# Attention with head pairs as units, and its first outputs moved inside SBUF into the next layer's input

## The chip, the cores and the metric

The kernel runs on one core of one Trainium2 chip. What counts is the device time of one execution in microseconds (us); a "run" is the median of its executions. The core has five engines that work beside each other, each through its own list of instructions: PE (TensorE: matmuls and transposes; PEld is its loading of weights), DVE (VectorE), ACT (ScalarE), POOL (GpSimd) and SP (SyncE), which in this kernel issues every DMA. Sixteen DMA engines carry the transfers between DRAM and SBUF, the on-chip memory of 128 partitions.

## What is computed

Three stages follow each other: a gated linear attention over 4 batches, 8 heads, 768 time steps and head dimension 48; a layer with a rational function; a layer with a cosine.

```python
for t in range(S):                       # attention, per batch and head
    state = alpha[:, :, t, :, None] * state + einsum('bhd,bhe->bhde', k[:, :, t], v[:, :, t])
    y[:, :, t] = einsum('bhd,bhde->bhe', q[:, :, t], state)
x = y.transpose(0, 2, 1, 3).reshape(B * S, H * D)          # 3072 tokens x 384
h = x @ w_in                                               # layer 1, 384 x 2048
P = a0 + a1*h + a2*h**2 + a3*h**3;  Q = 1 + |b0|*|h| + |b1|*h**2
x = (P / (Q + 1e-6)) @ w_out
h = x @ w_in2                                              # layer 2
return (h * cos(h)) @ w_out2
```

## The kernel before

Time is cut into NC = 6 chunks of C = 128 steps. A unit is one chunk of one batch: u = 4c + b, NU = 24 units in all. A tile of a unit has 128 partitions, two heads of a pair in rows 0 to 47 and 64 to 111 (the other rows are padding), and along the free axis four head pairs (HP = 4) of 128 steps. One slot of the attention loop (n from -3 to 24) carries several units, each in another stage: DVE makes the running product of alpha (`decay`) and its inverse, POOL scales q (L303, `scale_q`) and k (L298, `scale_k`) and masks the two score tiles (L323, `mask1`), PE computes scores, state and output, ACT copies out of PSUM. Each slot also splits one weight tile of the layers into a high and a low part (ACT L70, L71 and L195, DVE L75 and L76, POOL L205), since every float32 product of a layer is made of three products of such parts.

The output of a unit is copied out of PSUM by ACT (L400, `y_out`). For the first four units (chunk 0), the high part is rounded in that copy and DVE subtracts it from the PSUM value for the low part (L406, `y_lo`). `y_store` (L416) writes both to a DRAM buffer `x0d` (name in the trace `x`), 256 KB each; for units 4 and up the whole value goes to DRAM as `x0d` (name in the trace). High and low parts rest until then in tiles `kept` (`g`) and in rows of layer 1's input tile `y_rest` (`x`).

Layer 1's input of a block (one chunk of all four batches: 512 tokens) is three tiles of 128 of the 384 columns (kk), high and low. For block 0 both parts are read back from DRAM by `x_pieces`: `x_load(0, 0, kk)` makes a list of eight DMAs, which the attention loop issues one per slot from n = 8 (L1307): four over 128 partitions (256 KB) and four over 64 (128 KB). Rows in SBUF are 512 B at a time, since batches lie apart in DRAM. For blocks 1 to 5, `x_load` (L675) issues four DMAs at once; then ACT (L680) and DVE (L684) split the tile. The columns of layer 1 stand in an order in which heads of one parity follow each other, and the host orders the rows of w_in the same way (`by_pairs`).

All DMAs stand in one queue of SP, in the order of the code: in a slot the stores (L416), then loads of `a` (alpha, 258 KB), `kq` (k and q, 512 KB), one raw weight (L156, 384 KB; `raw` or `spare`), `v` (192 KB), then the x piece. A DMA also waits for the one that was issued eight before it. Layer 1 starts while the last units of attention are still worked on (slots LEAD = 20 and up): PE's products b<-x,w (L537), then the rational function on ACT, DVE and POOL (L603 to L624), then the second product (L553).

The loop of slots, as far as it bears on DMAs, follows with the functions.

Of the kernel before, what the change touches and what calls it, by code (L numbers as in the profile page):

```python
# [2 lines left out]

# [1 line left out]

# [5 lines left out]
F32 = mybir.dt.float32  # L11
F32R = mybir.dt.float32r
# [5 lines left out]
B, H, S, D = 4, 8, 768, 48  # L18
DM, DFF = 384, 2048
NC, C = 6, 128  # L20
HP = 4
NF = DFF // 128
NK = DM // 128
TB = B * C
# [16 lines left out]
def attn_then_two_moe(ctx, tc, kqT, aT, vP, w1i, w1o, ma, mb, w2i, w2o, out):  # L41
    nc = tc.nc
# [2 lines left out]
    dram = ctx.enter_context(tc.tile_pool(name="dram", bufs=1, space=bass.MemoryType.DRAM))  # L45

    xd = [dram.tile([NC, B, 128 * HP, C], F32, name="x0d"), dram.tile([NC, DM, TB], F32, name="x1d")]
    x0d = dram.tile([2, B, 128 * HP, C], F32, name="x0")
    wd = dram.tile([2 * NF, 128, 2, DM], F32, name="wd")
    wf = dram.tile([NF, 128, DM], F32, name="wf")  # L50

# [34 lines left out]
    wp = main.enter_context(tc.tile_pool(name="w", bufs=1))  # L86
# [26 lines left out]
    v_t = [const.tile([128, H * D + 64 - D], F32, tag=f"v{i}", name=f"v{i}") for i in range(4)]  # L113
    st_all = const.tile([128, 4, DM], F32, tag="st", name="st")

    ws = [[wp.tile([128, 2, DM], F32R, tag=f"w{s}_{i}", name=f"w{s}_{i}") for i in range(NF)] for s in range(2)]
    s_all = [const.tile([128, HP * D + 64 - D], F32, tag=f"s{b}", name=f"s{b}") for b in range(B)]
    s_c = [s[:, :HP * D].rearrange("p (a b) -> p a b", a=HP) for s in s_all]

# [6 lines left out]
    ready = set()  # L126
    spare = x_p.tile([128, 2, NK, TB], F32R, tag="x", name="spare").rearrange("p a b c -> p (a b c)").bitcast(I32)
    xt = {(0, 0): x_p.tile([128, 2, NK, TB], F32R, tag="x", name="x")}
    y_rest = xt[0, 0].rearrange("p a b c -> p (a b c)")
    raw64 = {}  # L130
    stage = {}
    LEAD = NU - 4
# [258 lines left out]
    def y_out(u):  # L391
        d = U[u]
        if u < NU - B:
            d["yo"] = kept[2 + u % 2]
            if 2 <= u < B:
                d["yo"] = y_rest[:, (2 + u) * TB:(3 + u) * TB].bitcast(F32).rearrange("p (a t) -> p a t", a=HP)
        else:
            d["yo"] = in_p.tile([128, HP, C], F32, tag="p", name="yo")
        out = d["yo"].bitcast(F32R) if u < B else d["yo"]
        nc.scalar.activation(out=out, in_=d["y"], func=AF.Copy)  # L400

    def y_lo(u):
        d = U[u]
        d["lo"] = y_rest[:, u * TB:(u + 1) * TB]
        yo = d["yo"].rearrange("p a t -> p (a t)")
        nc.vector.tensor_tensor(  # L406
            out=d["lo"], in0=d["y"].rearrange("p a t -> p (a t)"), in1=yo, op=ALU.subtract
        )

    def y_store(u, rest=False):  # L410
        c, b = divmod(u, B)
        if rest:
            to, t = x0d[1, b], U[u]["lo"].bitcast(F32)
        else:
            to, t = xd[0][c, b] if c else x0d[0, b], U[u]["yo"].rearrange("p a t -> p (a t)")
        nc.sync.dma_start(out=to.rearrange("(p a) t -> p (a t)", a=HP), in_=t)  # L416

    def convert(n, place):

# [232 lines left out]
    def x_load(m, blk, kk):  # L652
        if kk == 0 and (m, blk) not in xt:
            xt[m, blk] = x_p.tile([128, 2, NK, TB], F32R, tag="x", name="x")
        x = xt[m, blk][:, 1, kk, :].bitcast(F32)
        ks = slice(kk * 128, (kk + 1) * 128)
        pieces = []
        if m:
            nc.sync.dma_start(out=x, in_=xd[1][blk, ks, :])
        else:  # L660
            gap = (64 - D) * HP
            for p, row in {0: [(slice(0, 128), 0)], 1: [(slice(0, 64), 128), (slice(64, 128), 192 + gap)],
                           2: [(slice(0, 128), 256 + gap)]}[kk]:
                to_from = [(x, xd[0][blk])] if blk else [
                    (xt[0, 0][:, i, kk, :].bitcast(F32), x0d[i]) for i in range(2)
                ]
                for to, of in to_from:
                    rows = of[:, row:row + p.stop - p.start, :]
                    pieces.append(partial(
                        nc.sync.dma_start,  # L670
                        out=to[p].rearrange("p (b t) -> p b t", b=B), in_=rows.rearrange("b p t -> p b t")
                    ))
        if blk or m:
            for piece in pieces:
                piece()  # L675
        return pieces

    def x_hi(m, blk, kk):
        x = xt[m, blk]
# [586 lines left out]
    with tc.manual_schedule():  # L1266
        nc.scalar.preload_act_table_set("natural_log_exp_and_others")
        for name, u in (("a", 0), ("kq", 0), ("a", 1), ("a", 2), ("kq", 1)):
            load(u, name)
        nc.vector.memset(fresh, P_MIN)  # L1270
        nc.gpsimd.memset(ones, 1.0)
        nc.gpsimd.memset(half_pi, HALF_PI)
        nc.gpsimd.memset(lnb, LN_S * ONE_EPS)
        for t in v_t:
            nc.gpsimd.memset(t[:, H * D:], 0.0)
        nc.gpsimd.memset(ident, 1.0)
        nc.gpsimd.affine_select(
            ident, ident, pattern=[[1, 128]], compare_op=ALU.is_equal, fill=0.0, base=0, channel_multiplier=-1
        )
        for s in s_all:  # L1280
            nc.gpsimd.memset(s[:, HP * D:], 0.0)
        warm_up(13)
        x_pieces = [p for kk in range(NK) for p in x_load(0, 0, kk)]
        for n in range(-3, NU + 1):
            slot[0] = n
            if n == -1:
                load(3, "a")
                load(1, "v")
            if n >= 2:
                y_store(n - 2)  # L1290
            if 0 <= n - 3 < B:
                y_store(n - 3, True)
            if n >= -1:
                load(n + 5, "a")
            if n >= 0:
                load(n + 3, "kq")
                for i in range((min(n, 1) if n not in (0, 20) else 2) if n <= LEAD else 0):
                    w_fetch(2 * NF)
                load(n + 2, "v")
            if n == 3:  # L1300
                nc.sync.dma_start(out=cab[:, 0:4], in_=ma.unsqueeze(0).to_broadcast([128, 4]))
                nc.sync.dma_start(out=cab[:, 4:6], in_=mb.unsqueeze(0).to_broadcast([128, 2]))
            if n == 6:
                nc.scalar.activation(out=cq[:, 0:2], in_=cab[:, 4:6], func=AF.Abs)
                nc.scalar.activation(out=cq[:, 2:6], in_=cab[:, 0:4], func=AF.Copy, scale=-LN_S * LN_S)
            if n >= 8 and x_pieces:
                x_pieces.pop(0)()  # L1307
            if n == 1:
                warm_up(8)
            attention(n)  # L1310
            if n == -3:
                for name, u in (("v", 0), ("kq", 2)):
                    load(u, name)
            w_lo([nc.gpsimd])
            if n >= LEAD:
                layers(n - LEAD)
                y_out(n - 1)
        y_store(NU - 1)
        for n in range(NU + 1 - LEAD, F0):
            layers(n)  # L1320
        for k in range(SLOTS):
            threes(k)
        acc_out()
# [3 lines left out]
    def general():  # L1327
# [12 lines left out]
        with tc.For_i(0, NC, 1) as c:  # L1340
# [14 lines left out]
            for t in range(C):  # L1355
                v = two.tile([128, B, HP, D], F32, name="v")
                for j in range(2):
                    for b in range(B):
                        row = vP[one, b, t].rearrange("o (a j e) -> o j a e", a=HP, j=2)[:, j]
                        nc.sync.dma_start(out=v[64 * j:64 * j + 64, b], in_=row.to_broadcast([64, HP, D]))  # L1360
                w = two.tile([128, B, HP, D], F32, name="w")
                at = a[:, :, :HP].unsqueeze(3) if t == 0 else a_rest[:, :, :, t:t + 1]
                nc.vector.tensor_tensor(out=state, in0=state, in1=at.to_broadcast([128, B, HP, D]), op=ALU.mult)
                nc.vector.tensor_tensor(out=v, in0=v, in1=over_e(k, t), op=ALU.mult)
                nc.vector.tensor_tensor(out=state, in0=state, in1=v, op=ALU.add)
                nc.vector.tensor_tensor(out=w, in0=state, in1=over_e(q, t), op=ALU.mult)
                y = two.tile([2, B, HP, D], F32, name="y")
                for i in range(2):
                    p = psf.tile([2, 2, HP, D], F32, name=f"yp{i}")
                    nc.tensor.matmul(p, half, w[:, 2 * i:2 * i + 2], start=True, stop=True)  # L1370
                    nc.vector.tensor_copy(y[:, 2 * i:2 * i + 2], p)
                rows = yd[t].rearrange("b (a j e) -> j b a e", a=HP, j=2)
                for b in range(B):
                    nc.sync.dma_start(out=rows[:, b], in_=y[:, b])
            for b in range(B):
                yh = two.tile([128, DM], F32, name="yh")
                nc.sync.dma_start(out=yh, in_=yd[:, b, :])
                y = two.tile([128, DM], F32, name="yt")
                nc.vector.tensor_copy(y.rearrange("p (e a) -> p e a", a=HP), yh.rearrange("p (a e) -> p e a", a=HP))
                for kk in range(NK):  # L1380
                    p = psf.tile([128, 128], F32, name="tp")
                    nc.tensor.transpose(p, y[:, kk * 128:(kk + 1) * 128], ident)
# [124 lines left out]
```

## Time and profile before

| | us |
|---|---|
| runs (three) | 916.93, 918.09, 919.14 |
| median | 918.09 |
| profiled execution | 916.58 |
| its span | 914.9 |
| PE busy | 893.7 (98% of the span) |
| POOL, DVE, ACT busy | 710.0, 703.8, 695.5 |
| attention, until PE works without a gap | about the first 130 |

The granted TensorE clock is full in the whole span. The gaps of PE lie in the attention part. The DMA engines are full for about the first 115 us and a third busy after that. To read the profile, take the attention part apart from the layers: the wait that ends last before PE's continuous work says what a change in the attention part can move.

### The profile page before, as it was taken

Reading aid. Unit: us, or ns where it says so; the run is one execution under the profiler, and the core shown is the slowest. Engines: PE = TensorE matmul, PEld = TensorE weight load, DVE = VectorE, ACT = ScalarE, POOL = GpSimd, SP = SyncE. Lnnn points to the kernel's source line nnn. Section 1 sums busy time; section 2 is a strip of 40 time slices with the busy share of each in tenths; the row PEclk is TensorE's granted clock in tenths of the full one; section 3 lists DMA queues with packets and bytes.
Section 4 is the critical chain, followed back from the end, with each engine's and each line's share of the span. In section 5 each row is a group of like instructions: output and inputs, shape, how many; then the busy total and the mean of one; then the engine's idle time right before and its main releaser. Section 6 shows DMA issues by size and latency. Waiting matters only on the chain.

```text
span 914.9 us, 15676 instructions
## 1 busy us (share of the span) xinstructions
PE 893.7 (98%) x5348; PEld 740.6 (81%) x5348; DVE 703.8 (77%) x1247; ACT 695.5 (76%) x1302; POOL 710.0 (78%) x699
## 2 busy tenths in 40 slices
PE   7899989999999999999999999999999999999997
PEld 6787767888888888888888888878888888888885
DVE  8998789999899989979979968666367554555552
ACT  6998888888879788878778878756577666666653
POOL 7999999989789979879879767758887475655332
PEclk9999999999999999999999999999999999999999
DMA  9999840100234132232165467530243432533432
GB/s 324 388 380 379 331 132 18 31 22 18 69 113 121 44 126 74 78 121 87 41 190 195 153 209 252 196 120 27 69 139 104 155 123 89 171 104 104 139 104 90
DMA packets 67305, 128.83 MB, mean 141 GB/s; under 512 B 6928, under 2 KB 30224, under 8 KB 67216
## 3 DMA queue, kind: packets, MB, share of 16 engines
q1 hardware_dynamic: 67216, 127.74, 41.4%
q8 instruction: 44, 0.72, 0.3%
q14 instruction: 45, 0.37, 0.1%
HBM read 95.21 MB, written 32.51 MB: 140 GB/s over the span
## 4 chain that ended last, share of the span: by engine, by line
PE 86%; ACT 6%; DMA 3%; DVE 3%; issue 2%; POOL 0%; SPq 0%; ACTq 0%; DVEq 0%
PE b L537 28%; PE acc L553 28%; PE acc L1032 15%; PE b L997 6%; PE r L997 5%; DMA x0d<-g 1%; PE b L1176 1%; ACT hi L318 1%; ACT lo L318 1%; ACT r L275 1%; ACT st L70 1%; DMA kq<-kqT 1%; ACT g L336 1%; ACT w L195 1%; DVE p L260 1%
## 5 line engine op out<-in xcount | busy, mean ns | idle before, releaser
L537 PE MATMUL b<-x,w 128*128 128x512 f32 x1143 | 288.2, 396 | 2.5 <-DVE g L606 1.4
L537 PEld LDWEIGHTS b<-x,w 128*128 128x128 f32 x1143 | 214.3, 188 | 55.4 <-DVE g L606 2.0
L553 PE MATMUL acc<-hi,w 128*128 128x512 f32 x738 | 251.5, 395 | 0.0
L588 POOL TENSOR_TENSOR lo<-g,hi 128x512 fp32r<-128x512 f32 x128 | 173.5, 1355 | 70.0 <-ACT hi L583 63.7
L553 PEld LDWEIGHTS acc<-hi,w 128*128 128x128 f32 x738 | 138.7, 188 | 32.9
L1089 POOL TENSOR_TENSOR lo<-g,hi 128x512 fp32r<-128x512 f32 x64 | 83.0, 1297 | 103.6 <-ACT hi L1088 91.6
L553 PE MATMUL acc<-lo,w 128*128 128x512 f32 x369 | 146.2, 396 | 0.0
L583 ACT ACTIVATE hi<-g 128x512 fp32r<-128x512 f32 x128 | 80.6, 630 | 80.7 <-DVE g L619 43.4
L614 POOL TENSOR_TENSOR z<-z,ah 128x512 f32<-128x512 f32 x96 | 127.2, 1325 | 8.0
L1032 PE MATMUL acc<-hi,w_out 128*128 128x512 f32 x384 | 130.4, 396 | 0.0
L615 DVE TENSOR_TENSOR g<-g,b 128x512 f32<-128x512 f32 x96 | 65.3, 680 | 24.0 <-ACT g L612 23.4
L553 PEld LDWEIGHTS acc<-lo,w 128*128 128x128 f32 x369 | 69.4, 188 | 17.0
L1032 PEld LDWEIGHTS acc<-hi,w_out 128*128 128x128 f32 x384 | 68.7, 188 | 9.9
L1032 PE MATMUL acc<-lo,w_out 128*128 128x512 f32 x192 | 76.3, 397 | 0.4 <-POOL lo L1089 0.2
L613 POOL TENSOR_SCALAR z<-ah,cq 128x512 f32<-128x512 f32 x96 | 74.7, 778 | 2.1 <-ACT ah L611 2.1
L612 ACT ACTIVATE g<-b,cq 128x512 f32<-128x512 f32 x96 | 74.5, 776 | 0.0
L619 DVE SCALAR_TENSOR_TENSOR g<-g,cq,r 128x512 f32<-128x512 f32 x96 | 70.8, 738 | 0.1
L606 DVE SCALAR_TENSOR_TENSOR g<-g,cq,b 128x512 f32<-128x512 f32 x96 | 70.7, 736 | 0.0
L623 ACT ACTIVATE r<-z,lnb 128x512 f32<-128x512 f32 x96 | 66.7, 695 | 1.1 <-POOL z L614 1.1
L608 DVE SCALAR_TENSOR_TENSOR r<-z,r 128x512 f32<-128x512 f32 x96 | 65.6, 683 | 0.0
L603 DVE SCALAR_TENSOR_TENSOR z<-z,r 128x512 f32<-128x512 f32 x96 | 64.9, 676 | 0.0
L611 ACT ACTIVATE ah<-b 128x512 f32<-128x512 f32 x96 | 56.4, 587 | 7.5 <-PE b L537 7.3
(192 smaller groups left out, 1814.9 us busy)
## 6 DMA issues: line engine op xcount, KB each, us to landing
w_out<-wd SPq DMA_DIRECT2D x64, 384.0 KB, 3.0
kq<-kqT SPq DMA_DIRECT2D x24, 512.0 KB, 6.5
raw<-w2i SPq DMA_DIRECT2D x16, 384.0 KB, 3.5
w<-wd SPq DMA_DIRECT2D x16, 384.0 KB, 3.0
raw<-w2o SPq DMA_DIRECT2D x16, 384.0 KB, 3.3
wd<-w SPq DMA_DIRECT2D x16, 384.0 KB, 2.5
a<-aT SPq DMA_DIRECT2D x23, 258.0 KB, 5.7
v<-vP SPq DMA_DIRECT2D x24, 192.0 KB, 6.4
```

What stands on the lines that cost most here:

```text
L537: nc.tensor.matmul(h, ws[0][f][:, w, ks], x[:, xx, kk, :], start=i == 0, stop=i == 8)
L553: nc.tensor.matmul(acc[k], ws[1][f][:, w, ks], d[g], start=first and i == 0, stop=last and i == 2)
L583: nc.scalar.activation(out=t["hi"], in_=t["g"], func=AF.Copy)
L588: eng.tensor_tensor(out=t["lo"], in0=t["g"], in1=t["hi"].bitcast(F32), op=ALU.subtract)
L606: nc.vector.scalar_tensor_tensor(g, g, cq[:, 3:4], two["h"], ALU.add, ALU.mult)
L612: nc.scalar.activation(out=g, in_=h, func=AF.Identity, scale=cq[:, 5:6], bias=cq[:, 4:5])
L613: nc.gpsimd.tensor_scalar(zz, ah, cq[:, 1:2], cq[:, 0:1], ALU.mult, ALU.add)
L614: nc.gpsimd.tensor_tensor(out=zz, in0=zz, in1=ah, op=ALU.mult)
L619: nc.vector.scalar_tensor_tensor(g, g, cq[:, 2:3], r, ALU.add, ALU.mult)
L997: nc.tensor.matmul(tile[:, half], w[p], x[q], start=start and i == 0, stop=True, skip_group_check=True)
L1032: nc.tensor.matmul(acc[k], item["w"][:, w, ks], item[g], start=first, stop=last)
L1089: nc.gpsimd.tensor_tensor(out=p["lo"], in0=p["g"], in1=p["hi"].bitcast(F32), op=ALU.subtract)
```

## The change

Units are redrawn: a unit is now one chunk of one head pair, with the four batches along the free axis where the four head pairs stood (u = 4c + head pair). The host lays out q, k, alpha and v so, and w_in keeps its natural order (`by_pairs` is gone). Shapes and sizes of every tile and every load of the attention stay.

With that, a unit's tile holds, for each of two heads, 48 rows that belong together in layer 1's input. The first four units write their high and low parts (L400, L406) into `y_home`, the room of eight weights' tiles that are filled later (now one tile, `w_late`). A new function `y_move(u)`, called at n = u + 3, copies them from there into layer 1's input with DMAs from SBUF to SBUF, a high and a low row of 2 KB for each partition. `head_rows(h)` cuts a head's 48 rows where the boundary of 128 columns cuts them: 2, 3, 3, 2 DMAs in the four slots, of 48, 32 or 16 partitions (192, 128 or 64 KB). The eight stores of the first four units and the eight x pieces are gone. `x_load` for blocks 1 to 5 uses the same `head_rows`: ten DMAs of 48, 32 or 16 partitions with rows of 2 KB, in place of four.

```diff
-    x0d = dram.tile([2, B, 128 * HP, C], F32, name="x0")
-    ws = [[wp.tile([128, 2, DM], F32R, tag=f"w{s}_{i}", name=f"w{s}_{i}") for i in range(NF)] for s in range(2)]
+    ws = [[wp.tile([128, 2, DM], F32R, tag=f"w{s}_{i}", name=f"w{s}_{i}") for i in range((NF - 2 * B, NF)[s])] for s in range(2)]
+    w_late = wp.tile([128, 2 * B, 2, DM], F32R, tag="w0_8", name="w0_8")
+    ws[0] += [w_late[:, i] for i in range(2 * B)]
+    y_home = w_late.rearrange("p i a b -> p i (a b)")
...
-            if 2 <= u < B:
-                d["yo"] = y_rest[:, (2 + u) * TB:(3 + u) * TB].bitcast(F32).rearrange("p (a t) -> p a t", a=HP)
+            if u < B:
+                d["yo"] = y_home[:, 2 * u, :TB].bitcast(F32).rearrange("p (a t) -> p a t", a=HP)
...
-        d["lo"] = y_rest[:, u * TB:(u + 1) * TB]
+        d["lo"] = y_home[:, 2 * u + 1, :TB]
...
+    def head_rows(h):
+        for kk in range(NK):
+            e0, e1 = (min(max(kk * 128 + i - h * D, 0), D) for i in (0, 128))
+            if e0 < e1:
+                at = h * D + e0 - kk * 128
+                yield kk, slice(at, at + e1 - e0), slice(64 * (h % 2) + e0, 64 * (h % 2) + e1)
+
+    def y_store(u):
         c, b = divmod(u, B)
-        if rest:
-            to, t = x0d[1, b], U[u]["lo"].bitcast(F32)
-        else:
-            to, t = xd[0][c, b] if c else x0d[0, b], U[u]["yo"].rearrange("p a t -> p (a t)")
-        nc.sync.dma_start(out=to.rearrange("(p a) t -> p (a t)", a=HP), in_=t)
+        if c:
+            to = xd[0][c, b].rearrange("(p a) t -> p (a t)", a=HP)
+            nc.sync.dma_start(out=to, in_=U[u]["yo"].rearrange("p a t -> p (a t)"))
+
+    def y_move(u):
+        for h in (2 * u, 2 * u + 1):
+            for kk, to, of in head_rows(h):
+                nc.sync.dma_start(
+                    out=xt[0, 0][to, :, kk, :].bitcast(F32), in_=y_home[of, 2 * u:2 * u + 2, :TB].bitcast(F32)
+                )
...
-            for p, row in {0: [(slice(0, 128), 0)], 1: [(slice(0, 64), 128), (slice(64, 128), 192 + gap)],
-                           2: [(slice(0, 128), 256 + gap)]}[kk]:
...
+            for h in range(H):
+                for k, to, of in head_rows(h):
+                    if k == kk:
+                        rows = xd[0][blk, h // 2].rearrange("(p b) t -> p (b t)", b=B)
+                        nc.sync.dma_start(out=x[to], in_=rows[of])
...
-        x_pieces = [p for kk in range(NK) for p in x_load(0, 0, kk)]
...
             if 0 <= n - 3 < B:
-                y_store(n - 3, True)
+                y_move(n - 3)
...
-            if n >= 8 and x_pieces:
-                x_pieces.pop(0)()
...
     def slots(a, pad):
-        o[:, :, :, :D] = a.reshape(B, HP, 2, NC, C, D).transpose(3, 0, 2, 5, 1, 4)
+        o[:, :, :, :D] = a.reshape(B, HP, 2, NC, C, D).transpose(3, 1, 2, 5, 0, 4)
```

The order moves in three places of SP's queue. The first is slots 3 and 4. Before, from the two stores of slot 3 (high part in `g`, low part in `x`, both to DRAM) to the loads of slot 4:

```order
L416 DMA x_59<-g 128x512
L416 DMA x_59<-x 128x512
L237 DMA a<-aT 128x516
L237 DMA kq<-kqT 128x1024
L156 DMA raw<-w1i 128x768
L232 DMA v_102<-vP 128x384
L1301 DMA cab<-ma 128x4
L1302 DMA cab<-mb 128x2
L416 DMA x_59<-x 128x512 x2
L237 DMA a<-aT 128x516
L237 DMA kq<-kqT 128x1024
```

Now (`w_8_129` is `y_home`, `x` is layer 1's input in SBUF):

```order
L427 DMA x<-w_8_129 48x2x512 x2
L237 DMA a<-aT 128x516
L237 DMA kq<-kqT 128x1024
L156 DMA raw<-w1i 128x768
L232 DMA v_101<-vP 128x384
L1301 DMA cab<-ma 128x4
L1302 DMA cab<-mb 128x2
L427 DMA x<-w_8_129 32x2x512
L427 DMA x<-w_8_129 16x2x512
L427 DMA x<-w_8_129 48x2x512
L237 DMA a<-aT 128x516
L237 DMA kq<-kqT 128x1024
```

Two stores in each of these slots have become two or three moves at the same place, ahead of the slot's kq load. The second place is SP's queue in layer 1's slot 3, where the second block of x is loaded. Before:

```order
L416 DMA x0d<-yo 128x512 x2
L675 DMA x<-x0d 128x4x128
L675 DMA x<-x0d 64x4x128 x2
L675 DMA x<-x0d 128x4x128
L156 DMA raw<-w1o 128x768
L416 DMA x0d<-yo 128x512
```

Now:

```order
L422 DMA x0d<-yo 128x512 x2
L677 DMA x<-x0d 48x512 x2
L677 DMA x<-x0d 32x512
L677 DMA x<-x0d 16x512
L677 DMA x<-x0d 48x512 x2
L677 DMA x<-x0d 16x512
L677 DMA x<-x0d 32x512
L677 DMA x<-x0d 48x512 x2
L156 DMA raw<-w1o 128x768
```

Ten DMAs stand between the store and the raw weight where there were four. The third place is each slot from 8 to 15, where the x piece behind the load of v is gone from SP's queue. On PE, ACT, DVE and POOL the instructions of these slots keep their order.

## Rows read from the trace of the kernel before

**Rows 1.** Page, busy time: engine, us, share of the span, instructions.

```profile
PE 893.7 (98%) x5348; PEld 740.6 (81%) x5348; DVE 703.8 (77%) x1247; ACT 695.5 (76%) x1302; POOL 710.0 (78%) x699
```

**Rows 2.** Waits of PE, 129 us to the end: for whom, total us, times, longest.

```profile
PE b L537 <- DVE g L606: 1.4, 1, 1.4
PE acc L1032 <- POOL lo L1089: 0.2, 1, 0.2
```

**Rows 3.** Timeline of POOL: start us, length us, operation, idle time before and its releaser.

```profile
35.42 1.27 POOL L303 TENSOR_TENSOR kq<-kq,p 128x512 f32<-128x512 f32 x1
...
44.98 1.27 POOL L303 TENSOR_TENSOR kq<-kq,p 128x512 f32<-128x512 f32 x1
...
49.59 1.27 POOL L303 TENSOR_TENSOR kq<-kq,p 128x512 f32<-128x512 f32 x1
...
73.04 1.28 POOL L303 TENSOR_TENSOR kq<-kq,p 128x512 f32<-128x512 f32 x1 [0.37 <-DMA kq<-kqT]
...
78.21 1.28 POOL L303 TENSOR_TENSOR kq<-kq,p 128x512 f32<-128x512 f32 x1 [0.54 <-DMA kq<-kqT]
...
101.53 1.28 POOL L303 TENSOR_TENSOR kq<-kq,p 128x512 f32<-128x512 f32 x1
```

**Rows 4.** Timeline of ACT: two copies of outputs that follow each other.

```profile
65.84 0.60 ACT L400 ACTIVATE g<-b 128x512 f32<-128x512 f32 x1 [0.33 <-DMA x0d<-g]
...
71.01 0.60 ACT L400 ACTIVATE g<-b 128x512 f32<-128x512 f32 x1 [0.70 <-DMA x0d<-g]
```

**Rows 5.** Windows: stretch, length, busy us of each engine, clock, DMA share, GB/s.

```profile
49.00:60.00 11.00, 11.00 (x176) 9.31 (x174) 10.56 (x28) 10.94 (x25) 11.00 (x13) 1.00 1.06 400
60.00:80.00 20.00, 18.79 (x288) 15.49 (x284) 18.11 (x49) 18.27 (x39) 19.09 (x22) 1.00 1.06 355
80.00:90.00 10.00, 8.96 (x139) 7.47 (x141) 8.52 (x23) 9.24 (x19) 9.93 (x11) 1.00 1.06 397
```

**Rows 6.** DMAs issued by SP: start us, issue us; below each its KB and us to landing.

```profile
38.06 0.42 SPq L237 DMA_DIRECT2D kq<-kqT  x1
...
kq<-kqT SPq DMA_DIRECT2D x1, 512.0 KB, 6.8
```

**Rows 7.** DMAs issued from 48.9 to 88.6 us: count, KB each, median us to landing.

```profile
x<-x SPq DMA_DIRECT2D x4, 256.0 KB, 6.0
x<-x SPq DMA_DIRECT2D x4, 128.0 KB, 6.3
```

**Rows 8.** Timeline at the start of layer 1, SP, ACT, DVE and PE.

```profile
119.83 2.38 SPq L675 DMA_DIRECT2D x<-x0d  x4
122.32 0.44 SPq L156 DMA_DIRECT2D raw<-w1o  x1
...
126.92 0.55 ACT L70 ACTIVATE st<-raw 128x384 f32<-128x384 f32 x1 [0.29 <-DMA raw<-w1o]
...
127.95 0.56 DVE L75 SCALAR_TENSOR_TENSOR st<-st,raw 128x384 int32<-128x384 int32 x1 [1.88 <-ACT raw L71]
...
129.82 1.43 PE L537 MATMUL b<-x,w 128*128 128x512 f32 x5 [1.36 <-DVE g L606]
```

**Rows 9.** Chain that ended last, 115 to 131 us: start, us, what.

```profile
122.32 4.58 DMA raw<-w1o
```

**Rows 10.** Issue pace of three loads in layer 2; raw loads issued alone (156.57, 205.64).

```profile
477.05 1.37 SPq L659 DMA_DIRECT2D x<-x1d  x3
...
raw<-w1i SPq DMA_DIRECT2D x1, 384.0 KB, 2.9
...
raw<-w1o SPq DMA_DIRECT2D x1, 384.0 KB, 3.3
```

**Rows 11.** Timeline at the load of the third block of x.

```profile
231.85 0.63 ACT L680 ACTIVATE x<-x 128x512 fp32r<-128x512 f32 x1 [4.21 <-DMA x<-x0d]
...
233.72 0.74 DVE L606 SCALAR_TENSOR_TENSOR g<-g,cq,b 128x512 f32<-128x512 f32 x1
...
234.98 1.33 PE L537 MATMUL b<-x,w 128*128 128x512 f32 x5
```

More of the change, by code (lines that the diff above doesn't have):

```diff
@@ L1 @@
 from contextlib import ExitStack
-from functools import partial
 import numpy as np
@@ L128, in attn_then_two_moe @@
     xt = {(0, 0): x_p.tile([128, 2, NK, TB], F32R, tag="x", name="x")}
-    y_rest = xt[0, 0].rearrange("p a b c -> p (a b c)")
     raw64 = {}
@@ L408, in y_lo @@
         )
-    def y_store(u, rest=False):
-        c, b = divmod(u, B)
-        if rest:
-            to, t = x0d[1, b], U[u]["lo"].bitcast(F32)
-        else:
-            to, t = xd[0][c, b] if c else x0d[0, b], U[u]["yo"].rearrange("p a t -> p (a t)")
-        nc.sync.dma_start(out=to.rearrange("(p a) t -> p (a t)", a=HP), in_=t)
+    def head_rows(h):
[5 more added lines that the diff above has]
+    def y_store(u):
+        c, b = divmod(u, B)
+        if c:
[7 more added lines that the diff above has]
+                )
     def convert(n, place):
@@ L656, in x_load @@
         ks = slice(kk * 128, (kk + 1) * 128)
-        pieces = []
         if m:
@@ L660, in x_load @@
         else:
-            gap = (64 - D) * HP
-            for p, row in {0: [(slice(0, 128), 0)], 1: [(slice(0, 64), 128), (slice(64, 128), 192 + gap)],
-                           2: [(slice(0, 128), 256 + gap)]}[kk]:
[L664 to L676, printed above, removed]
+            for h in range(H):
[3 more added lines that the diff above has]
+                        nc.sync.dma_start(out=x[to], in_=rows[of])
     def x_hi(m, blk, kk):
@@ L1374, in general @@
                     nc.sync.dma_start(out=rows[:, b], in_=y[:, b])
+            yh = fb.tile([128, HP, B, 2, D], F32, name="yh")
+            nc.sync.dma_start(out=yh.rearrange("p h b j e -> p h (b j e)"), in_=yd)
             for b in range(B):
-                yh = two.tile([128, DM], F32, name="yh")
-                nc.sync.dma_start(out=yh, in_=yd[:, b, :])
                 y = two.tile([128, DM], F32, name="yt")
-                nc.vector.tensor_copy(y.rearrange("p (e a) -> p e a", a=HP), yh.rearrange("p (a e) -> p e a", a=HP))
+                for h in range(H):
+                    nc.vector.tensor_copy(y[:, h * D:(h + 1) * D], yh[:, h // 2, b, h % 2])
                 for kk in range(NK):
@@ L1476 @@
     q, k, v, alpha = (np.asarray(inputs[n]) for n in ("q", "k", "v", "alpha"))
-    vp = np.ascontiguousarray(v.reshape(B, H, NC, C, D).transpose(2, 0, 3, 1, 4)).reshape(NC, B, C, H * D)
+    vp = np.ascontiguousarray(v.reshape(B, HP, 2, NC, C, D).transpose(3, 1, 4, 0, 2, 5)).reshape(NC, B, C, H * D)
     def w_in(w):
         return np.ascontiguousarray(w.reshape(NK, 128, NF, 128).transpose(2, 1, 0, 3)).reshape(NF, 128, DM)
-    def by_pairs(w):
-        return w.reshape(HP, 2, D, DFF).transpose(1, 2, 0, 3).reshape(DM, DFF)
     arrays = {
@@ L1489 @@
         "vP": vp,
-        "w1i": w_in(by_pairs(np.asarray(inputs["moe_w_in"]).view(np.int64))),
+        "w1i": w_in(np.asarray(inputs["moe_w_in"]).view(np.int64)),
         "w1o": np.ascontiguousarray(inputs["moe_w_out"]).view(np.int64).reshape(NF, 128, DM),
```

## The prediction, made before the changed kernel ran

> **What bounds the kernel now.** I read the busy times first: PE is busy for 98% of the span [rows 1]. Then the waits of PE from 129 us to the end: two, one of 1.4 us that ends at 129.82 us and one of 0.2 us [rows 2]. So after 129.8 us the kernel costs what its matmuls cost, the change takes out or adds no matmul, and a microsecond won or lost before PE turns continuous is one of the total. The question is when that moment comes.
>
> In the attention part that precedes it, POOL's rows repeat a pattern of five operations: the scaling of q (L303) to the next L303 takes 4.61 us when nothing is waited for (44.98 to 49.59) and POOL has no gap [rows 3]. ACT's L400 follows itself after 5.17 us (65.84 to 71.01), of which 0.70 is a wait for a store [rows 4]; without it 4.47, so POOL sets the pace, narrowly. The load of k and q (kq) puts L303 off at 73.04 and 78.21, by 0.37 and 0.54 us. The starts tell the whole: 35.42 to 44.98 is 9.56 us for two units, 0.34 over 2 x 4.61; 44.98 to 101.53 is 56.55 us for twelve, 1.23 over 12 x 4.61 [rows 3]. 1.57 us is all that better transfers can win there.
>
> The transfers are full: the DMA engines' share is 1.05 to 1.06 [rows 5], and the rate 400 and 397 GB/s where all transfers span 128 partitions (49 to 60, 80 to 90 us). One unit needs a, kq, a weight and v, 1.38 MB (258 + 512 + 384 + 192 KB of 1024), and with a store of 256 KB it is 1.64 MB, 4.1 us at 400 GB/s: 0.5 us inside POOL's 4.61. The kq load issued at 38.06 lands 6.8 us later, at 44.9, and its L303 starts at 44.98: no slack [rows 3, 6].
>
> **Early stores and moves (slots 3 to 6).** Eight stores of 256 KB go (four high, four low parts, L416), and ten moves come, 1.573 MB, each over 48, 32 or 16 partitions with rows of 2 x 2 KB. All of either stand ahead of the kq load issued at 38.06 (slot 6). They wait for the same ACT and DVE instructions as the stores did; the two further issues cost SP some 0.5 us each (pace below), in slots of 4.6 us with seven issues. Counting bytes, 2.097 - 1.573 = 0.524 MB less stand before it, 1.31 us at 400 GB/s. That is a gain on this queue, but POOL can use only 0.34 of it.
>
> No row shows a transfer inside SBUF, nor one over 48 partitions. The nearest rows are the pieces of x that the kernel already loads (L1307). Four of 256 KB over 128 partitions run in the two stretches of full rate: no excess over their bytes, so that is the low end; a gain beyond the bytes is excluded because the engines are full already. The four of 128 KB over 64 partitions run from 60 to 80 us, at 355 GB/s [rows 5, 7]. Against 400 these 20 us lack 0.9 MB, 2.25 us, 0.56 us for each of the four beyond its own 0.33 us. By bytes, the moves are twelve such pieces: 0 to 6.8 us of excess. They are nearer to the narrow end, since none covers more than 48 partitions. But they come in twos from opposite halves of the partitions (a head of each half), where the 64-row pieces stand alone in a slot, and their rows are 2 KB, not 512 B. I take two thirds of 0.56, 0.38 us a move, 3.8 us for ten. Then the kq load of slot 6 comes 3.8 - 1.31 = 2.5 us late, and as it has no slack POOL's L303 is 2.5 us late, with the masks and the scaling of k queued behind it, then scores on PE, and the rest of attention. Afterwards the queue gains 0.5 us per unit, so no later kq waits, but POOL cannot run faster than 4.61: the 2.5 us stay. **+2.5 us.**
>
> The Trainium skill ("SBUF — State Buffer", section "Door 1: The DMA port swizzle (why `[64,N]` ≈ `[32,N]`)") says that partitions 0 to 63 reach only half of the 16 ports, so that a narrow transfer gets about half the rate, some 218 GB/s. By an estimate from that figure the moves take 7.2 us instead of 3.9, an excess of 3.3 us, and the sum below would be 0.5 us less; the 64-row pieces here took more than that page has them take (0.89 us for 128 KB, 147 GB/s), so the trace agrees in direction, not in size.
>
> **Late pieces (slots 8 to 15).** Eight loads of x pieces go, 1.573 MB, with the excess just found. They are what makes kq late at 73.04 and 78.21 (0.37 and 0.54 us of wait, right in the slow stretch [rows 3, 5]) and they hold back the stores on which ACT's copies wait (0.70 us at 71.01, L400 [rows 4]). Without them the unit's transfers are 4.1 us. POOL gets its 1.23 us. **-1.2 us.**
>
> **Load of the second block of x (L675).** At 119.83 SP issues four DMAs in 2.38 us, and only then the raw weight at 122.32, which lands 4.58 us later; ACT, which splits it, starts at 126.92, then L71, DVE's L75, L603 and L606, and PE at 129.82: the last chain before PE is continuous [rows 8, 9]. Ten DMAs stand there now. Issues back to back go at 0.46 us (three in 1.37 us [rows 10]) to 0.6 (four in 2.38), so ten take 4.7 and the raw weight is issued 2.2 us later. The landing need not follow: a raw load alone lands in 2.9 to 3.3 us [rows 10], and here 4.58, because 786 KB of x are in the way; issued later it finds more of them done. 122.3 + 2.2 + (2.9 to 3.3) = 127.4 to 127.8, against 126.9. Bounds: -0.3 (the narrow pieces with 2 KB rows clear faster than those of 512 B) and +2.2 (4.58 stays). I take **+0.7 us**; nothing covers it, as DVE idles 1.88 us for L71 there and PE 1.36.
>
> The same load at 228.88 takes ten DMAs too; ACT waits 4.21 us for x there, but DVE's L606 ends at 234.46 and PE uses it at 234.98 [rows 11]: 0.5 us of slack against 0 to 0.3 more. Later ones come with more time. Nothing.
>
> **Edits at nothing.** High and low parts are written by the same ACT and DVE instructions (L400, L406), in another tile; the order of the work on PE, ACT, DVE and POOL and what each waits for on another engine stay. The room is that of weights that are written several slots later, long after the moves landed. The first layer reads x at 104 us at the earliest, 55 us after the last move. Layouts and the order of w_in are made by the host; bytes of k, q, alpha, v are the same. The fallback isn't run.
>
> **Sum.** +2.5 - 1.2 + 0.7 = +2.0 us: the profiled execution of 916.58 us (span 914.9) becomes 918.6. It lies 1.5 below the median of 918.09, so 920.1 for a median.
>
> **Rivals.** (a) **The moves cost only their bytes.** Then kq is no longer late: -0.34 - 1.23 + 0.7 = -0.9, 917.2; with the x load at its low end -1.9, 916.2. For it: half the bytes' way is inside the chip, and transfers of opposite halves may run side by side. Against it: the 64-row pieces. The balance tips at a total excess of 1.8 us, 0.18 a move. (b) **The moves cost what the narrow pieces did**, 6.8 us, with kq of slot 6 late by 5.5: +5.5 - 1.2 + 0.7 = +5.0, 923.1; slower. It decides by how little of the pairs overlaps: from 3.7 us of excess in all (0.37 a move, just under what I take) the change is slower by more than 0.2%. For it: the pieces are narrower than 64; against it, the pairs and the longer rows. The Trainium skill (same page, section "Can I just issue two DMAs to hit both halves?") says that two transfers over opposite halves run one after the other, with some 6% to gain, which speaks for this rival against my two thirds; no run so far shows it. (c) **The ten issues decide**: the raw weight lands 2.2 us later, not 0.7: +3.5, 921.6, and with (b) +6.5, 924.6. For it: the 4.58 us; against it, that the load would wait for the same bytes at a later time.
>
> **How the numbers follow.** Forecast 0.42 (around 918.9 to 921.3), (a) 0.30, (b) and (c) together 0.28. Changes of 0.2%, 1.84 us, are about what a measurement of this kernel tells from none: faster is below 916.25, slower above 919.93. Most of (a) lies inside that, its low end outside: faster 0.16. The forecast is cut by the upper bound: half same. Same is then 0.2 from the forecast and 0.2 from (a) and the low ends of (c): 0.40; slower 0.44. The range goes from (a)'s low end to (b) with a dear x load: 916.0 to 924.5.
>
> **What would show it.** Right: POOL's L303 that follows the last move waits 2 to 3 us for kq, in one or two units, and has no wait after 50 us; the DMA rate in slots 3 to 6 falls to some 300 GB/s and is about 400 from 55 to 100; L675 takes 4 to 5 us and ACT's L70 after it starts 7.5 to 8 us after the first of the ten. PE continuous comes at 131.8 instead of 129.8. Wrong: no wait for kq at all near 45 us (rival a), one of 5 us (b), a raw load that still takes 4.6 us (c), or PE waiting again after it is continuous, or a time that moves without that moment.

## Result and the profile after

The changed kernel takes 923.12 us (median of 6; 922.21 to 925.52) against 918.1 of the kernel before: a ratio of 1.0066, interval 1.0051 to 1.0081. By the medians it is slower by 5.0 us (the ratio would make it 6.1); forecast were 2.0. The profiled execution took 925.52 us with a span of 923.4, 8.5 more than the one of before, so it is longer than the median by some 2.4 us. A second profile of the same kernel (`after_again`, 922.51 median) has a span of 920.6. What the two share is told below.

First the waits of POOL from 15 to 110 us, in the kernel after; they answer the two waits of [rows 3]:

```profile
POOL kq L303 <- DMA kq<-kqT: 5.5, 3, 2.9
POOL hi L323 <- ACT hi L318: 0.7, 1, 0.7
POOL kq L298 <- DVE r L259: 0.6, 1, 0.6
```

All 5.5 us of waiting for kq lie in the slots of the moves; POOL's timeline there:

```profile
30.86 1.29 POOL L303 TENSOR_TENSOR kq<-kq,p 128x512 f32<-128x512 f32 x1
...
36.75 1.27 POOL L303 TENSOR_TENSOR kq<-kq,p 128x512 f32<-128x512 f32 x1 [1.25 <-DMA kq<-kqT]
...
44.25 1.26 POOL L303 TENSOR_TENSOR kq<-kq,p 128x512 f32<-128x512 f32 x1 [2.87 <-DMA kq<-kqT]
...
50.29 1.27 POOL L303 TENSOR_TENSOR kq<-kq,p 128x512 f32<-128x512 f32 x1 [1.42 <-DMA kq<-kqT]
```

The last of them is the L303 that started at 44.98 before. Behind it no kq is late any more. The windows (stretch, length, busy times, clock, DMA share, GB/s) show the queue in the slots of the moves, PE starved, its clock a little later, and the stretch where the 64-row pieces had been [rows 5]:

```profile
21.00:31.00 10.00, 7.73 (x126) 6.43 (x128) 9.72 (x25) 9.91 (x22) 10.00 (x13) 1.00 1.04 316
31.00:41.00 10.00, 9.30 (x152) 7.85 (x148) 9.46 (x26) 9.33 (x22) 8.75 (x10) 1.00 0.87 262
41.00:46.00 5.00, 3.09 (x49) 2.41 (x47) 3.19 (x8) 2.65 (x6) 2.13 (x3) 1.00 1.03 320
51.00:60.00 9.00, 9.00 (x79) 7.37 (x76) 6.72 (x21) 5.58 (x12) 9.00 (x11) 0.50 1.04 409
```

The DMA engines are busy (shares of 0.87 to 1.04) and move only 262 to 320 GB/s; as soon as the moves are through it is 409. PE worked 3.09 of the 5 us from 41 to 46, and from 51 to 60 its granted clock is 0.50, the lower level of 1.2 GHz. ACT then waits for PE (1.22 and 1.57 us), DVE for ACT (1.80 us), POOL for both (the waits of 0.7 and 0.6 us above): two more units come 1.4 us late in all.

```profile
56.14 0.60 ACT L318 ACTIVATE hi<-sc 128x512 f32<-128x512 f32 x1 [1.22 <-PE sc L311]
...
59.90 0.60 ACT L400 ACTIVATE g<-b 128x512 f32<-128x512 f32 x1 [1.57 <-PE b L386]
```

In the second profile PE idles in these slots too (3.85 of the 5 us from 41 to 46 worked), and its clock stays at 1.00.

At the start of layer 1, the timeline of SP, ACT and PE (it answers [rows 8]):

```profile
125.19 4.58 SPq L677 DMA_DIRECT2D x<-x0d  x10
129.88 0.37 SPq L156 DMA_DIRECT2D raw<-w1o  x1
...
133.46 0.54 ACT L68 ACTIVATE st<-raw 128x384 f32<-128x384 f32 x1 [1.46 <-DMA raw<-w1o]
...
136.33 3.90 PE L550 MATMUL b<-x,w 128*128 128x512 f32 x9 [2.51 <-DVE g L619]
```

The ten DMAs take 4.58 us to issue; the raw weight lands 3.6 us after its issue, and ACT takes it up at 133.46; PE waits 2.51 us in place of 1.36. And the nine matmuls behind that wait take 3.90 us, where they took 2.37 in the profile before: the granted clock from 125 to 140 us is 0.89 (1.00 before).

```profile
125.00:140.00 15.00, 12.49 (x95) 9.53 (x92) 11.64 (x17) 11.50 (x23) 12.64 (x12) 0.89 0.52 160
```

The 8.5 us of the two profiles are then: +5.31 up to the L303 of 44.98; +0.13 from there to the one of 101.53 (the clock's 1.41 and the 1.28 that the missing late pieces give back); +1.07 to PE's continuous work; +1.99 behind it, of which the nine matmuls at the lower clock are 1.53. The second profile reads 4.13 - 1.24 + 0.65 + 2.16 = 5.70.

### The profile page after: what moved, and what is told of

Its sections match the earlier page's. It is cut to its first block, busy times and chain, and to the rows that moved or that the text cites. A ratio compares the mean times of both kernels' runs of the same rounds, so it can differ in the third digit from the quotient of the medians.

```text
span 923.4 us, 15728 instructions
## 1 busy us (share of the span) xinstructions
PE 901.9 (98%) x5348; PEld 747.3 (81%) x5348; DVE 703.5 (76%) x1247; ACT 695.7 (75%) x1302; POOL 709.6 (77%) x699
## 4 chain that ended last, share of the span: by engine, by line
PE 84%; POOL 5%; DMA 5%; ACT 2%; DVE 2%; SPq 1%; issue 1%; ACTq 0%; DVEq 0%
PE b L550 28%; PE acc L566 28%; PE acc L1033 15%; PE b L998 6%; PE r L998 5%; DMA spare<-w1i 2%; POOL kq L298 1%; POOL kq L303 1%; POOL w L205 1%; DMA kq<-kqT 1%; PE b L1177 1%; DMA a<-aT 1%; DMA cab<-ma 1%; POOL hi L323 1%; POOL lo L323 1%
## 5 line engine op out<-in xcount | busy, mean ns | idle before, releaser
L619 DVE SCALAR_TENSOR_TENSOR g<-g,cq,b 128x512 f32<-128x512 f32 x96 | 70.6, 736 | 0.0
L616 DVE SCALAR_TENSOR_TENSOR z<-z,r 128x512 f32<-128x512 f32 x96 | 64.9, 676 | 0.0
```

The lines of the kernel that those rows point to most:

```text
L619: nc.vector.scalar_tensor_tensor(g, g, cq[:, 3:4], two["h"], ALU.add, ALU.mult)
```

## Experiments

Two theories stood against each other on the moves: they are slow because each covers few partitions (width), or because ten small transfers take the eight places in SP's queue, so that the kq load is issued late (number). In the changed kernel the kq load issued at 33.07 us came right after the landing, at 33.01, of the raw weight that stood eight DMAs ahead of it, so the second could not be put aside by reading. Two more questions were the discount for opposite halves and the price of the ten loads. The table has, for every profile, three starts of POOL's L303 (named by the time they have in the profile before), the start of PE's continuous work, and the span; the runs' medians stand in the text. Each ratio is against the kernel before in the same job (medians 918.3 to 918.9 us).

| profile | 30.82 | 44.98 | 101.53 | PE continuous | span |
|---|---|---|---|---|---|
| before | 30.82 | 44.98 | 101.53 | 129.82 | 914.9 |
| before_raw | 30.88 | 45.80 | 103.00 | 131.20 | 917.7 |
| before_wide | 31.76 | 47.38 | 102.68 | 130.55 | 916.2 |
| after | 30.86 | 50.29 | 106.97 | 136.33 | 923.4 |
| after_again | 30.97 | 49.11 | 104.42 | 133.36 | 920.6 |
| raw_first | 32.77 | 50.72 | 106.00 | 133.62 | 919.1 |
| x_load4 | 31.44 | 48.71 | 103.99 | 131.56 | 917.9 |
| few_moves | 30.85 | 49.22 | 104.52 | 133.33 | 920.4 |
| cab_first | 32.06 | 48.63 | 104.11 | 133.09 | 920.4 |
| same_half | 31.67 | 51.34 | 106.56 | 136.15 | 922.7 |
| wide_moves | 30.83 | 46.74 | 102.25 | 130.76 | 917.3 |
| spread | 30.90 | 44.72 | 100.63 | 129.23 | 916.3 |
| spread_raw | 30.88 | 44.70 | 100.02 | 127.61 | 912.9 |

One thing in it limits all that follows: where the first slots are the same code (the three rows of before; or after, after_again, raw_first and x_load4), the L303 of 44.98 still differs by 2.0 to 2.4 us from execution to execution. A single profile settles nothing finer than that.

**Width: the moves made wide.**

```diff
-                    out=xt[0, 0][to, :, kk, :].bitcast(F32), in_=y_home[of, 2 * u:2 * u + 2, :TB].bitcast(F32)
+                    out=flat[:, 384 * h + c0:384 * h + c1].bitcast(F32), in_=y_home[:, h, c0:c1].bitcast(F32)
```

> The changed kernel with its ten moves made wide: each still goes from SBUF to SBUF, at the same place of SP's queue and with the same bytes (192, 128 or 64 KB), but over 128 partitions with rows of 1536, 1024 or 512 B. (Block 0 of layer 1's input then holds other rows than it should.) Two theories on the 5.5 us that POOL's L303 waits for kq in the changed kernel. Narrow: a transfer over 48 partitions or fewer runs far below the full rate, so the wide moves cost only their bytes; kq waits fall from 5.5 us to 0 to 0.5, the DMA rate from 21 to 41 us rises from 262 to 316 back to 380 or more, time 917.5 to 918.5. Queue places: each DMA waits for the one issued eight before, and ten moves in place of eight stores leave fewer bytes under way; it doesn't matter how wide they are, waits stay 4 to 5.5 us, time 922 to 923.

Measured: 920.14 us, ratio 1.0012 (0.9998 to 1.0026), against 1.0066 and 1.0058 of the changed kernel. The waits for kq fall from 5.5 and 4.2 us in the two profiles of the changed kernel to:

```profile
POOL kq L303 <- DMA kq<-kqT: 2.2, 3, 1.1
```

The same ten places, bytes and path inside SBUF cost some 3 us less when the rows span all partitions (L303 at 46.74, against 49.71 as the mean of four profiles with the narrow moves). The rows are shorter as well, 1536 B or less in place of 2 KB; before_wide, below, changes the width at rows of equal length. The time fell short of the 917.5 to 918.5 expected: 2.2 us of waits are left, and the rate from 31 to 41 us is 305 GB/s, not 380. before_wide has 307 there with plain stores, so this rate by itself is no sign of the moves.

**Number: five moves for ten, at the same bytes per slot.**

```diff
+            0: [(slice(0, 48), slice(0, 1024), slice(0, 48), 0), (slice(48, 96), slice(0, 1024), slice(64, 112), 0)],
+            1: [(slice(0, 48), slice(1024, 3072), slice(0, 48), 0)],
+            2: [(slice(48, 96), slice(1024, 3072), slice(64, 112), 2)],
+            3: [(slice(96, 128), slice(0, 3072), slice(0, 32), 2)],
```

> The changed kernel with its ten moves replaced by five that carry the same bytes in each slot (2 x 192, 384, 384, 384 KB), over 48, 48, 48, 48 and 32 partitions. (They bring other rows to block 0.) It separates width from number. Width: the kq waits stay at 3.4 to 5.5 us, the ninth unit after the first loads (the L303 that started at 44.98 us before) starts between 48.7 and 50.7 us as in the four profiles of the changed kernel's own moves, time 921.5 to 923. Number (each DMA waits for the one eight before, and ten small ones leave few bytes under way): waits fall to 0 to 2 us, that L303 starts near 46 to 47, 919 to 920.

Measured: 924.89 us (four executions, 1.9 us above the 921.5 to 923 expected for width), ratio 1.0075 (1.0055 to 1.0095); L303 at 49.22, as expected; the waits, with the DMA engines busy throughout (1.03 to 1.05 from 21 to 51 us):

```profile
POOL kq L303 <- DMA kq<-kqT: 4.4, 3, 1.6
```

Half as many DMAs, and nothing won: the width decides, and no effect of the number is seen. The idle share that spoke for the number (0.87 from 31 to 41 us in the first profile) is 0.99 in after_again, whose time is the same.

**Number again: the two tiny loads of `cab`, which stood ahead of the moves of slot 4, put before the attention.**

```diff
+        nc.sync.dma_start(out=cab[:, 0:4], in_=ma.unsqueeze(0).to_broadcast([128, 4]))
+        nc.sync.dma_start(out=cab[:, 4:6], in_=mb.unsqueeze(0).to_broadcast([128, 2]))
         nc.vector.memset(fresh, P_MIN)
...
-            if n == 3:
-                nc.sync.dma_start(out=cab[:, 0:4], in_=ma.unsqueeze(0).to_broadcast([128, 4]))
-                nc.sync.dma_start(out=cab[:, 4:6], in_=mb.unsqueeze(0).to_broadcast([128, 2]))
```

> The changed kernel with the two tiny loads of layer 1's constants (cab, 2 and 1 KB, between slots 3 and 4) moved to the beginning, ahead of attention. Narrow theory: they carry no bytes worth counting, so nothing changes: POOL waits 5.5 us for kq, 923. Queue places: the kq load of slot 4, which was issued at 33.07 us just after the load eight before it had landed at 33.01, is issued two places and some 2 us earlier, DMA share from 31 to 41 us rises from 0.87 to 1, waits fall to about 3.5 us, time 921.

Measured: 924.74 us, ratio 1.006 (1.0039 to 1.008), no gain. Its profile looks more like what was expected for the number: waits of 2.6 us, a DMA share of 1.03 from 31 to 41 us, and L303 at 48.63, or 16.57 us after its own one of 30.82, where the changed kernel's four profiles have 17.27 to 19.43. The time shows none of it. Alone this run would decide nothing, and a small part of the number isn't excluded; few_moves speaks against a large one.

**Opposite halves.**

```diff
-                    out=xt[0, 0][to, :, kk, :].bitcast(F32), in_=y_home[of, 2 * u:2 * u + 2, :TB].bitcast(F32)
+                    out=xt[0, 0][to, :, kk, :].bitcast(F32), in_=y_home[of.start % 64:of.start % 64 + of.stop - of.start, 2 * u:2 * u + 2, :TB].bitcast(F32)
```

> The changed kernel with both heads of a unit moved out of the same rows of SBUF (0 to 47) in place of rows of opposite halves (0 to 47 and 64 to 111); where they go to is unchanged. (Odd heads' rows of block 0 then hold the even heads' values.) It tests the discount of the prediction, that two moves of opposite halves run partly side by side. If they do, taking the halves together costs 1.5 to 3 us more on top of the changed kernel: 925 to 926. If each move goes by its own width and they follow each other, nothing changes: 923.

Measured: 923.67 us, ratio 1.0047 (1.0031 to 1.0064), beside 922.51 and 1.0058 of the changed kernel in the same job: longer by the medians, shorter by the ratios, so no difference clear of the noise. L303 at 51.34 is 0.6 us beyond the latest of the changed kernel's four, less than their scatter of 2.0 us. The waits:

```profile
POOL kq L303 <- DMA kq<-kqT: 5.8, 3, 3.1
```

So no run shows an overlap of halves that could be lost, and that ground of the prediction's discount finds no support. Only the rows read were changed here; those written to were the same in both kernels. The Trainium skill says the same ("SBUF — State Buffer", section "Can I just issue two DMAs to hit both halves?"): two such transfers follow each other.

**The late pieces, in the kernel before.** The four pieces over 64 partitions became four over 128 with half the columns.

```diff
+                    if not blk and kk == 1:
+                        half = slice(0, 2) if p.start == 0 else slice(2, 4)
+                            nc.sync.dma_start, out=to.rearrange("p (b t) -> p b t", b=B)[:, half],
+                            in_=of[half, 128:256, :].rearrange("b p t -> p b t")
```

> The kernel before with its four pieces of x over 64 partitions made into four over 128 partitions with half the columns (two batches), 128 KB as before and at the same places. (The middle third of block 0's input then has its rows in another order.) Narrow theory: the rate from 60 to 80 us rises from 355 to about 400 GB/s, L303's waits of 0.37 and 0.54 us at 73 and 78 us go, and the kernel gains 1.0 to 1.2 us: 917.0. If the number of DMAs or the load of the slots decided, nothing changes: 918.1.

Measured: 917.02 us, ratio 0.9977 (0.9963 to 0.999). The rate of the stretch in question:

```profile
60.00:80.00 20.00, 19.21 (x298) 15.88 (x298) 18.65 (x48) 19.37 (x41) 20.00 (x24) 1.00 1.06 400
```

400 GB/s in place of 355 [rows 5], and 55.30 us from the L303 of 44.98 to that of 101.53 in place of 56.55. At the same bytes, the same rows of 512 B and the same number of DMAs, 64 partitions cost the kernel 1.25 us by these two profiles, 1.7 us by the medians (917.0 was expected).

**The ten loads of the second block.**

```diff
-            for h in range(H):
-                for k, to, of in head_rows(h):
...
+            for to in [slice(0, 64), slice(64, 128)] if kk == 1 else [slice(0, 128)]:
+                nc.sync.dma_start(out=x[to], in_=rows[to])
```

> The changed kernel with four DMAs in the loads of blocks 1 to 5 of x (128, 64, 64, 128 partitions, rows of 2 KB) in place of ten. (They bring other rows of the same buffer.) If the ten issues delay the raw weight behind them, it is issued some 2.2 us after the first of the four instead of 4.7, and PE is continuous 1.0 us earlier: 922.0. If the ten cost nothing because the weight would be late anyway: 923.1.

Measured: 921.12 us, ratio 1.0023 (1.0008 to 1.0039). From the L303 of 101.53 to PE's continuous work it takes 27.57 us; in the seven profiles that keep the ten loads with the weight behind them it takes 28.51 to 29.59, in the three of the kernel before 27.87 to 28.29. The four loads are wider than the ten as well; that the issues delay the weight is seen in its own issue, 2.37 us after the first of the loads instead of 4.69, and ACT no longer waits for it. The gain is larger than the 1.1 us expected, and PE shows why: it waits 1.35 us instead of 2.5, and its clock holds.

```profile
131.56 2.37 PE L550 MATMUL b<-x,w 128*128 128x512 f32 x9 [1.35 <-DVE g L619]
```

**The weight ahead of the ten loads.**

```diff
             if n > 0:
                 w_fetch(2 * NF)
+                if n == 3:
+                    for kk in range(NK):
+                        x_load(*nxt, kk)
...
-        if nxt != (1, 2) and load:
+        if nxt != (1, 2) and load and n != 3:
```

> The changed kernel with the raw weight of layer 1's slot 3 issued ahead of the ten DMAs of the second block of x. If the ten issues delay PE through that weight, PE's last wait falls from 2.5 us to 0 to 0.5 (the weight lands some 3 us after the store ahead of it), and with it goes the clock's drop on the nine matmuls behind: -2.0 us without a drop, -3.5 with one, 919.6 to 921. If the second block of x then comes too late, ACT's L693 waits and PE with it, and nothing is won.

Measured: 920.24 us, ratio 1.002 (1.0011 to 1.003), 2.3 us less than after_again in the same job. 27.62 us from the L303 of 101.53 to PE, as with four loads. The expected wait of 0 to 0.5 us was wrong: 1.38 are left, and they end by another chain, ACT's and DVE's own work (L195, L68, L69, then L73, L616, L619). No load stands in it.

```profile
133.62 2.36 PE L550 MATMUL b<-x,w 128*128 128x512 f32 x9 [1.38 <-DVE g L619]
```

**The same in the kernel before.** The edit is the one just shown, in `layers` of the kernel before, with its four DMAs.

> The kernel before with the raw weight of layer 1's slot 3 issued ahead of the four DMAs of the second block of x. In the prediction the landing of that weight was what PE waited for last. If so, and alone, it gains up to 1.4 us (PE's last wait goes). With the changed kernel the same edit left a wait of 1.38 us, ended by the chain of ACT and DVE (L195, L68, L69, L73, L616, L619), so I expect the two to be level in the kernel before: -0.3 to 0 us, 918.6.

Measured: 918.57 us, ratio 0.9998 (0.9985 to 1.0011). The weight that ended the chain in [rows 9] was level with ACT's and DVE's chain: it set the time by 0.29 us (ACT's idle time in [rows 8]) at most, and PE's last wait only goes from 1.36 to 1.21 us. A chain of waits names the last to come, not how far behind the next one was.

**The moves spread out,** one in each of the slots 3, 4, 5, 6, 8, 10, 12, 14, 16 and 18; in `spread_raw` with the weight first as well.

```diff
-                y_move(n - 3)
+                moves.extend(y_moves(n - 3))
+            if n in (3, 4, 5, 6, 8, 10, 12, 14, 16, 18):
+                moves.pop(0)()
```

> The changed kernel with its ten moves spread over slots 3, 4, 5, 6, 8, 10, 12, 14, 16 and 18, one each, and the raw weight of layer 1's slot 3 ahead of the x load. If the moves are slow by their width but the queue has 0.5 us to spare per slot (1.1 without a store), the kq waits shrink from 5.5 us to 0 to 1.5 and PE's last wait to 0.5: -1.6 to -0.1 in attention, -1.0 at the start of layer 1, 916 to 917.5, faster than both kernels. If the narrow moves stop the queue wherever they stand, the waits only spread with them: 920 to 921.

> The changed kernel with its ten moves spread over slots 3, 4, 5, 6, 8, 10, 12, 14, 16 and 18, and nothing else. Against the version that also issues the raw weight of layer 1's slot 3 first (915.2) it parts what each of the two is worth. The waits for kq should be gone as there; PE's last wait is 2.3 to 2.8 us again in place of 1.4, so 1.1 us more where the clock holds, 2 to 2.5 where it falls behind that wait: 916.3 to 917.5.

Measured: `spread_raw` 915.19 us, ratio 0.9969 (0.9954 to 0.9984); `spread` 918.38, ratio 1.0004 (0.9991 to 1.0017). The first is 0.8 us better than expected, the second 0.9 us worse. In `spread_raw` no wait of POOL from 15 to 110 us is left. The moves still slow the queue (326 to 363 GB/s from 21 to 60 us), but a slot has room for one of them. L303 comes at 44.70 and 100.02, 0.28 and 1.51 us earlier than before: nearly all of the 1.57 us that the prediction gave as the most to be won there. `spread` has 0.5 us of waits and the long last wait of PE with its clock:

```profile
129.23 3.10 PE L550 MATMUL b<-x,w 128*128 128x512 f32 x9 [2.44 <-DVE g L619]
```

`spread_raw` at the same place:

```profile
127.61 2.37 PE L550 MATMUL b<-x,w 128*128 128x512 f32 x9 [1.36 <-DVE g L619]
```

The two spans differ by 3.4 us: 0.6 in attention, 1.0 at that wait, and 1.8 behind it. `spread_raw` beats both kernels: in its own job 915.19 stands against 918.86 of the one before and 922.51 of the changed one.

## Why the prediction was right and where it was not

The direction and the places were right, and 923.12 us lies inside the range given, near its upper end; but +5.0 us is two and a half times the forecast.

- **What bounds the kernel: right but for the clock.** Every difference arose before PE turned continuous or followed from the wait just before it. But not all of it came before: some 1.2 us came behind that moment, where the prediction held that the kernel costs what its matmuls cost. They cost more while the granted clock was at its lower level.
- **Early term: right in kind, too small.** The sum has +2.5 us; the two profiles of the changed kernel show +5.31 and +4.13. The term that was mis-sized is the excess of the moves, 3.8 us. Over means of the same first slots, the L303 of 44.98 comes at 49.71 us with the moves (four profiles) and at 46.05 with the stores (three): 3.7 us, uncertain by about 1 us since each group scatters by 2.0 to 2.4 (counted from each profile's own L303 of 30.82 it is 3.3). With the 1.31 us of saved bytes that is an excess of 5.0 us, 0.50 a move. One error lies in the working: the bound of 6.8 us counts the moves by bytes, as twelve pieces, but the discounted price was multiplied by ten; two thirds of 6.8 would have been 4.5. The 0.5 us that are then still missing lie within the scatter: three quarters of the bound were measured, two thirds taken. The reason given first for the discount, pairs from opposite halves, is the one that same_half does not bear out; the other, longer rows, no run tests. That the waits come in three units (1.25, 2.87, 1.42 us) and not in one or two adds up the same.
- **What the early term rests on: shown.** Width, by wide_moves against few_moves: same bytes, the first with ten wide, the second with five narrow DMAs; and by before_wide, at equal rows and number. The half rate that the Trainium skill gives for a narrow range ("SBUF — State Buffer", "Door 1: The DMA port swizzle (why `[64,N]` ≈ `[32,N]`)") led to an estimate of 3.3 us of excess; the runs agree in kind and lie above it.
- **Late term: right.** -1.2 forecast; 55.3 us in before_wide, after_again and spread_raw, in place of 56.55 (and 57.20 in before_raw). In the first profile the clock hid it.
- **Second block's load: right in size, not in consequence.** +0.7 forecast, +1.07 and +0.65 in the two profiles, the weight landing in 3.6 us (2.9 to 3.3 taken). Missing is what came on PE behind the longer wait: in all six profiles with a last wait of 2.44 us and more, and in none of the seven with 2.35 or less, the nine matmuls behind took 3.1 to 3.9 us instead of 2.37. From PE's continuous work to the end it is 786.6 to 787.3 us in those six and 785.1 to 786.5 in the seven, by means 1.2 us more. With the wait shortened in raw_first and x_load4 the clock held; after 2.35 us in wide_moves it held too, so the length of the wait alone is not shown to decide.
- **Sum.** By means of the profiles: +3.7 for the moves, -1.25 for the late pieces, +0.85 for the ten loads (28.97 us against 28.12 in the kernel before) and +1.2 for the clock behind them, 4.5 against 5.0 measured; a second fall of the clock, at 46 to 61 us, comes in some executions only. The time is the one that rival (b) gave, but not for its reason alone: its 5.5 us for the moves were too much, and the clock, which stood in no sum, made up the rest. That it gives the measured 923.1 is luck. Rival (c) did not come: the weight landed sooner, not 4.58 us after its issue.
- **Edits at nothing: right.** No wait for the moved data or its room appeared; PE waits once more in the rest of the span, 0.2 us, as before.

## What to carry to other kernels

In this kernel a transfer over part of the partitions cost its bytes and an excess (some 0.5 us a move), and the bytes saved (1.31 us in all) didn't pay for it where the queue was full and the next load had no slack. Move the time of such transfers before you change their shape: one per slot, the same ten moves cost nothing here (no wait of POOL in `spread_raw`, L303 at 44.70 and 100.02 us). And issue what the critical engine waits for ahead of a long list of DMAs, even if the list's data are needed soon.

## What the runs showed that was not expected

- A wait of PE can cost more than its length. After last waits of 2.44 to 2.83 us the granted clock fell (0.89 over 125 to 140 us) and took 0.7 to 1.5 us more on the next nine matmuls alone; after 1.2 to 1.4 us it never did, nor after the 2.35 us of wide_moves. A gain or loss at such a wait can be worth twice its size: raw_first won 2.3 us by shortening it by 1.1 to 1.35.
- With the same code in the first slots, the moment at which the load of k and q arrives scatters by 2 us between executions, at nearly full DMA shares; plain stores moved 377 GB/s from 31 to 41 us in one profile and 307 in another (shares 1.03 and 0.97).
